# An attention and DFT kernel: eleven spectral blocks beside attention instead of ten, a thinner output projection, and more tiles for loads

## The chip, the cores and the metric

The kernel runs on one core of a Trainium2 chip. The metric is the device time of one launch in microseconds. The engines are TensorE (PE, with PEld for its weight loads), VectorE (DVE), ScalarE (ACT), GpSimd (POOL) and SyncE (SP), which here issues nearly all DMAs. Each engine runs its own instructions in the order in which the kernel emits them; a DMA that has to wait for a buffer holds up whatever stands behind it in its issuer's queue.

## The reference

Two mixers see the same `x` (2048 rows of 512), and a gate adds them:

```python
qkv = x @ wqkv                                  # 32 heads of 16
p = softmax(q @ k.T * 16 ** -0.5)               # 2048 x 2048 per head
a = (p @ v).reshape(2048, 512) @ wo
b = dft_seq_re @ (x @ dft_hid_re.T) - dft_seq_im @ (x @ dft_hid_im.T)
g = sigmoid((x * gate_w).sum(-1))
out = g * a + (1 - g) * b
```

All of it is float32. The weights of the attention are large, so the softmax needs a row maximum that is right before the exponentials are taken, and products are made from a high and a low part of each operand (three matmuls for one product).

## The kernel before

**Two parts.** The *front* makes the projections (q, k, v), the two hidden DFTs and most of the DFT along the sequence ("spectral" blocks), and beside them part of the *scans*: matmuls of q and k whose only result is the row maximum. The second part is *attention*, 512 steps (16 pairs of heads, two halves of the queries, 16 blocks of keys). Each step makes scores (`qk`, L214), exponentials on ACT (L238 for the first half of the columns, L246 twice for the second) and the products with the values (`pv`, L758).

**What fills the steps of attention.** A step has room for other work on PE. Step 2 to step `MIX - 1` hold one scan each (`next_scan`). From `MIX` on, `next(fill)` runs the generator `outputs()`: first `LATER` spectral blocks of the second DFT half, 16 steps each with three pairs of matmuls a step (`spectral`); then the output projection `mix_heads` for 16 row blocks t, each in two steps (4 and 5 pairs) or, for even t below `2 * SLOW`, in four (2, 2, 2, 3 pairs); then twelve steps of `mix_some`. There are 1024 scans in all; `FRONT` of them are made in the front, so `MIX = TOTAL - FRONT + 1`. Step numbers below are these steps; a step's place in its pair of heads is called i, as in the code (0 to 31).

**Slots.** Every product in the front is a pair of matmuls on the two halves of the PE rows (`halves_of`, L189), and after each the kernel calls `beside()`. One such call is a *slot*. Twelve slots make one projection, or a quarter u of a spectral block. The front before has 80 projections and 88 quarters (`coef`: 64 of the first DFT half, 24 of the second), 2016 slots. `beside` adds `1 / pace` per slot and emits a scan whenever the sum reaches one: `PACE`, `SUMS` in the projections, `BESIDE` once folding has begun, `PART` in the spectral part, `SWAP` at its start and where the DFT half changes. `after(n, f)` emits work n slots later, which is how the casts, the stores and the loads are spread.

**Scans in the front.** From scan 64 on they are folded (`scan_folded`, L158): for one half of the keys ACT takes `Relu` of the difference of two key blocks (L162), for the other DVE adds it and takes the maximum (L164). Each uses one of four PSUM banks, so a late ACT or DVE stops PE at the next scan with that bank. The order of pairs is `SEQ`: the ten pairs of `EARLY`, then the first `FRONT % 64` scans of `PART_PAIR` (11), then pair 10. The rows of a pair (q and k, two tiles of the pool `stk`, which has six buffers) are loaded by eight DMAs, seven slots apart, when the scan listed in `ROWS` is reached.

**The swap of operands.** The spectral products read operands `ah[s]`, `al[s]`, s = 0 to 15. During t = 15 of the first half (four quarters of `coef`, slots 1656 to 1680 and 1704 to 1728) each is replaced by the second half's: `renew(s)` casts the raw operand on ACT (L701), then a subtraction on DVE or POOL follows, and for s >= 8 the next raw operand is ordered (`load_operand`, L342, tag `raw`). The raw operands 0 to 7 come in two `stk` tiles named `early`, ordered from slot 1584 on. The coefficients of quarter n are loaded by `fetch` (L361, tag `craw`) and split on POOL by `prepare` three quarters ahead (L368, L369).

**Near the end of the front**, eight quarters before its last, the rows of `PART_PAIR` are loaded once more for the scans of attention, and those of pair 0 for `qk` (`load_use`). In attention `load_use(p + 1)` comes at i = 18 and `load_scan` ten scans before a pair's last. `output_rows(c)` loads the heads' results for four row blocks of the output projection, `load_y(c)` the rows of the spectral sum that they are added to.

Of the kernel before, what the change touches and what calls it, by code (L numbers as in the profile page):

```python
# [10 lines left out]
F32 = mybir.dt.float32  # L11
# [7 lines left out]
P = 128  # L19
S = 2048  # L20
D = 512
# [3 lines left out]
NB = S // P  # L25
# [4 lines left out]
CS = 4  # L30
NU = NB // CS
PERIODS = 2 * NB
SCANS = 64
TOTAL = SCANS * NP
LATER = 10
FRONT = 564 + 16 * LATER
FOLDED = range(SCANS, FRONT)
PACE, SUMS, BESIDE, PART, SWAP = 3.9, 5.2, 2.72, 2.07, 2.97
PART_PAIR = FRONT // SCANS
EARLY = [0, 4, 5, 6, 7, 1, 2, 3, 8, 9]  # L40
SEQ = [(p, i) for p in EARLY for i in range(SCANS)]
SEQ += [(PART_PAIR, i) for i in range(FRONT % SCANS)] + [(p, i) for p in range(len(EARLY), PART_PAIR) for i in range(SCANS)]
SEQ += [(n // SCANS, n % SCANS) for n in range(FRONT, TOTAL)]
ROWS = {SCANS * n + (20 if n else 40): p for n, p in enumerate(EARLY[1:])}
ROWS.update({SCANS * len(EARLY) - 60: PART_PAIR, SCANS * len(EARLY) - 34: len(EARLY)})
NWARM = 20
MIX = TOTAL - FRONT + 1
OUT = MIX + NB * LATER
SLOW = 3
SCANS_IN = 0  # L50
AHEAD = (30, 31, 37, 44)


def build(tc, xT, wqkv, wo, wrT, wiT, cr, ci, gate, out):
    nc = tc.nc
    with ExitStack() as ctx:
# [176 lines left out]
        def qk_both(p, h, kb):  # L233

            ps = wide(1 - SCANS_IN, "s3")
            qk(p, h, kb, 0, [ps[:, j, :] for j in range(2)])
# [18 lines left out]
        with ExitStack() as pf:  # L255
# [36 lines left out]
            def beside():  # L292
# [5 lines left out]
                pace[1] += 1.0 / pace[0]  # L298
                while seen[0] < FRONT and pace[1] >= 1.0:
                    pace[1] -= 1.0  # L300
# [37 lines left out]
                engine.tensor_sub(lo, raw, hi.bitcast(F32))  # L338

            def load_operand(ph, s, pool):  # L340
                raw = pool.tile([P, D], F32, tag="raw", name="abr", bufs=3)
                nc.sync.dma_start(raw, ab_d[ph][s])  # L342
                return raw

# [6 lines left out]
            for ph, plain, pair in ((0, range(NB - 2), (NB - 2, NB - 1)), (1, range(2, NB), (0, 1))):  # L351
                split_up = [(ph, t, u) for half in range(2) for t in pair for u in (2 * half, 2 * half + 1)]
                whole = [(ph, t, u) for t in plain for u in range(NU)]
                coef += split_up + whole if ph else whole + split_up
            coef = coef[:len(coef) - NU * LATER]
            craw, ready = {}, {}

            def load_coef(n, raw):
                ph, t, u = coef[n]
                craw[n] = raw  # L360
                nc.sync.dma_start(raw, (cr, ci)[ph][t, :, u * CS:(u + 1) * CS, :])  # L361
# [273 lines left out]
            with ExitStack() as py:  # L635
                cp = py.enter_context(tc.tile_pool(name="cp", bufs=2, reuse_waits="tile"))
                def fetch(n):
                    if n < len(coef):
                        load_coef(n, cp.tile([P, CS, P], F32, tag="craw", name="craw", bufs=5))

                for n in range(4, 8):
                    fetch(n)
                for d in range(4):
                    after(4 + 6 * d, split_operand, NB - 4 + d, tail[:, d, :], nc.gpsimd)
                scan_at(SWAP)
                after(24, scan_at, PART)
                pss, yre, early = {}, {}, {}

                def go_ahead(k):

                    if k == 0:
                        assert seen[0] == FRONT, (seen, pace)
                        scanned.update(unfolded)
                        sums.append(narrow("k1", "pvb"))
                        nc.vector.memset(sums[0], 0.0)
                    if k == 1:
                        e = next_eb()
                        ahead.append(qk_single(0, 0, 0, [e[:, j, :] for j in range(2)]))
                    elif k == 2:
                        scan(seen[0], wide(1 - SCANS_IN, "s1"))  # L660
                        seen[0] += 1
                    else:
                        ahead.append(qk_both(0, 0, k // 3))

                def mixed(ph, t, yre, tx, ty):
                    y = cp.tile([P, D], F32, tag="y", name="y")
                    nc.gpsimd.tensor_add(y, tx, ty)
                    if ph:
                        nc.gpsimd.tensor_add(y, y, yre)
                    after(14, nc.sync.dma_start, y_d[t // 4][:, t % 4, :], y)  # L670

                for n, (ph, t, u) in enumerate(coef):
                    prepare(n + 3)
                    fetch(n + 8)
                    if u == 0 and (ph, t) == (0, NB - 1):
                        scan_at(SWAP)
                    if u == 2 and (ph, t) == (1, 0):
                        scan_at(PART)
                    if n == len(coef) - 2 * NU:
                        unfolded[PART_PAIR], loads = row_loads(PART_PAIR, nc.sync)  # L680
                        for load in loads:
                            load()
                        load_use(0)
                    hi, lo = ready.pop(n)
                    if u == 0:
                        pss[t] = xy()
                        if ph:
                            yre[t] = cp.tile([P, D], F32, tag="yre", name="yre")
                            nc.sync.dma_start(yre[t], y_d[t // 4][:, t % 4, :])
                    if (ph, t, u) == (0, NB - 3, 0):  # L690
                        for i in range(2):
                            raw = stk.tile([P, 4, D], F32, tag="stk", name="early")
                            for d in range(4):
                                early[4 * i + d] = raw[:, d, :]
                                after(24 * i + 6 * d, nc.sync.dma_start, raw[:, d, :], ab_d[1][4 * i + d])
                    swap = (ph, t) == (0, NB - 1)

                    def renew(s):
                        raw = early.pop(s)
                        ah[s], al[s] = block(2 * s), block(2 * s + 1)  # L700
                        nc.scalar.copy(ah[s], raw)  # L701
                        after(4, (nc.gpsimd if s % 4 == 3 else nc.vector).tensor_sub, al[s], raw, ah[s].bitcast(F32))
                        if s >= 8 and s + 3 < NB:
                            early[s + 3] = load_operand(1, s + 3, cp)

                    for w in range(CS):
                        s = u * CS + w
                        for i, (c_, a_) in enumerate(((hi, ah[s]), (hi, al[s]), (lo, ah[s]))):
                            halves_of(pss[t], c_[:, w, :], a_, s == 0 and i == 0, s == NB - 1 and i == 2)
                            beside()  # L710
                            if n >= len(coef) - NU and 3 * s + i in AHEAD:
                                go_ahead(AHEAD.index(3 * s + i))
                        if swap:
                            if s == 7:
                                for i in range(8, 11):
                                    early[i] = load_operand(1, i, cp)
                            after(1 + 5 * (s % 8), renew, s)
                    if u == NU - 1:
                        tx = cp.tile([P, D], F32, tag="tx", name="tx")
                        last = n == len(coef) - 1  # L720
                        ty = cp.tile([P, D], F32, tag="raw" if last else "ty", name="ty", bufs=3 if last else 2)
                        if last:
                            for v, ps in zip((tx, ty), pss[t]):
                                nc.vector.tensor_scalar_mul(v, ps, gm[:, t:t + 1])
                        else:
                            nc.scalar.mul(tx, pss[t][0], gm[:, t:t + 1])
                            after(5, nc.scalar.mul, ty, pss[t][1], gm[:, t:t + 1])
                        after(10, mixed, ph, t, yre.get(t), tx, ty)
                run_due((True, True))

        assert seen[0] == FRONT + 1 and turns[0] % 2 == SCANS_IN, (seen, turns)

        with ExitStack() as pa:
# [12 lines left out]
            def pair_banks():  # L746
                return wide(SCANS_IN, "s1")

# [109 lines left out]

            raws, units = [], [(t, u) for t in range(NB - LATER, NB) for u in range(NU)]
            parts = []  # L860
# [84 lines left out]
            def outputs():  # L945

                for t in range(NB - LATER, NB):
                    yield from spectral(t)
                for c in range(NC):
                    for t in range(4 * c, 4 * c + 4):  # L950
                        yield from mix_heads(t, (2, 2, 2, 3) if t < 2 * SLOW and t % 2 == 0 else (4, 5))
                    if c < 2:
# [41 lines left out]
            for step in range(NP * PERIODS):  # L994
                p, i = step // PERIODS, step % PERIODS
# [120 lines left out]
```

## Time and profile before

| | us |
|---|---|
| median of 3 runs | 1736.33 |
| lowest, highest | 1735.86, 1737.74 |
| the profiled execution | 1736.52 |
| its span in the profile | 1734.7 |

In the profile the front ends at about 670 us, the scans in attention at about 1245 us, the spectral blocks beside attention at about 1597 us. Rows of stretches give, after the stretch and its length, each engine's busy time with its number of instructions, then the clock of TensorE, the share of the DMA engines and GB/s. In rows of waits stand the total, the count and the longest wait; in rows of the chain the start, the length, and the engine with its line; in rows of the timeline the start, the length, and in brackets the idle time before with what ended it.

### The profile page before, as it was taken

The numbers are of one execution on the slowest core, as the hardware profiler recorded it, in microseconds if no ns is written. First come the engines' busy times: TensorE is split into PE (matmuls) and PEld (weight loads), VectorE is DVE, ScalarE is ACT, GpSimd is POOL, SyncE is SP. The second block draws the span as 40 slices with busy tenths as digits, with TensorE's granted clock in tenths as the row PEclk, the third lists the DMA queues.
The fourth block names the chain that finished last, engine by engine and source line by source line (L and its number), as shares of the span: only waits on it lengthen the run. The fifth ranks groups of instructions, "written<-read, shape, count | busy, mean of one in ns | idle before, by whom it ended". The sixth has DMA issues, their size and how long they took to land.

```text
span 1734.7 us, 36067 instructions
## 1 busy us (share of the span) xinstructions
PE 1718.8 (99%) x13676; PEld 1045.2 (60%) x13676; DVE 1094.3 (63%) x2065; ACT 1507.4 (87%) x2487; POOL 648.9 (37%) x770
## 2 busy tenths in 40 slices
PE   9999999999999999999999999999999999999998
PEld 7978888889888786433333333333455555555554
DVE  6898888899999897666666666666512222122333
ACT  5447888888888788999999999999988888888885
POOL 3673335755555662223323232332322322223221
PEclk9999999999999999999999999999999999999999
DMA  7783457433336746043333332351333244254712
GB/s 255 243 279 75 147 159 214 141 108 115 105 114 192 160 117 114 21 84 62 61 61 64 59 75 51 56 100 43 60 86 92 68 115 89 67 149 138 177 36 99
DMA packets 123710, 193.03 MB, mean 111 GB/s; under 512 B 54112, under 2 KB 56656, under 8 KB 116624
## 3 DMA queue, kind: packets, MB, share of 16 engines
q1 hardware_dynamic: 84464, 170.20, 37.3%
q0 software_dynamic: 38496, 19.47, 5.5%
q8 instruction: 107, 1.75, 0.5%
q10 hardware_dynamic: 576, 1.05, 0.2%
q14 instruction: 67, 0.55, 0.1%
HBM read 129.63 MB, written 61.61 MB: 110 GB/s over the span
## 4 chain that ended last, share of the span: by engine, by line
PE 94%; POOL 1%; DMA 1%; issue 1%; ACT 1%; DVE 1%; SPq 0%; DVEq 0%; POOLq 0%; ACTq 0%
PE pvb L758 28%; PE xy L189 23%; PE s L214 19%; PE s L189 10%; PE s L158 9%; PE s L139 5%; POOL s L282 1%; DMA abr<-ab_d 0%; POOL el L282 0%; ACT fold L162 0%; DMA raws<-wqkv 0%; DVE fold L164 0%; DVE y L856 0%; PE s L556 0%; ACT eh L282 0%
## 5 line engine op out<-in xcount | busy, mean ns | idle before, releaser
L238 ACT ACTIVATE eb<-s 128x1024 f32<-128x1024 f32 x512 | 575.6, 1124 | 65.7 <-PE s L214 65.4
L246 ACT ACTIVATE e<-s 128x512 f32<-128x512 f32 x1022 | 605.6, 702 | 0.4 <-PE s L214 0.4
L141 DVE TENSOR_REDUCE mx<-s 128x2 f32<-128x1024 f32 x364 | 442.5, 1225 | 188.9 <-PE s L139 188.7
L758 PE MATMUL pvb<-eb,va 128*17 128x512 f32 x2052 | 513.0, 597 | 0.0
L758 PE MATMUL pvb<-e,va 128*17 128x512 f32 x2044 | 512.1, 597 | 0.0
L164 DVE CUSTOM_DVE_ANT_0 fold<-s,fold 128x512 f32<-128x512 f32 x660 | 442.6, 690 | 57.4 <-PE s L158 20.3
L162 ACT ACTIVATE fold<-s 128x512 f32<-128x512 f32 x660 | 387.4, 603 | 74.7 <-PE s L158 52.0
L214 PEld LDWEIGHTS s<-qs,ks 50*128 50x128 f32 x2048 | 211.9, 184 | 355.6 <-ACT eb L238 255.1
L214 PE MATMUL s<-qs,ks 50*128 50x512 f32 x2048 | 420.0, 434 | 0.0
L189 PE MATMUL xy<-b,c 64*128 64x512 f32 x2448 | 400.6, 393 | 1.0 <-ACT s L478 0.7
L158 PE MATMUL s<-ks,qs 48*128 48x512 f32 x1320 | 323.3, 406 | 4.3 <-ACT fold L162 3.1
L189 PEld LDWEIGHTS xy<-b,c 64*128 64x128 f32 x2448 | 288.2, 187 | 17.1 <-ACT s L478 2.8
L158 PEld LDWEIGHTS s<-ks,qs 48*128 48x128 f32 x1320 | 178.2, 184 | 52.4 <-ACT fold L162 13.9
L777 POOL DMA_DIRECT2D r_d<-lc x31 | 18.1, 583 | 456.5 <-DVE lc L776 456.5
L758 PEld LDWEIGHTS pvb<-eb,va 128*17 128x17 f32 x2052 | 70.5, 96 | 192.3 <-issue 185.1
L139 PE MATMUL s<-ks,qs 48*128 48x512 f32 x728 | 151.2, 395 | 0.7 <-DVE mx L141 0.7
L770 POOL DMA_DIRECT2D lc<-ob x124 | 62.9, 514 | 154.9 <-DVE ob L767 154.5
L189 PE MATMUL xy<-w,b 64*128 64x512 f32 x768 | 116.9, 393 | 0.2 <-ACT s L478 0.2
L369 POOL TENSOR_TENSOR c<-craw,c 128x512 fp32r<-128x512 f32 x84 | 110.6, 1317 | 6.7
L189 PE MATMUL s<-b,chi 64*128 64x512 f32 x670 | 105.9, 392 | 0.3 <-ACT chi L1071 0.3
L368 POOL CAST c<-craw 128x512 fp32r<-128x512 f32 x84 | 51.9, 618 | 126.6 <-PE xy L189 121.6
L189 PEld LDWEIGHTS xy<-w,b 64*128 64x128 f32 x768 | 83.9, 186 | 11.0 <-ACT s L478 1.1
(138 smaller groups left out, 1478.8 us busy)
## 6 DMA issues: line engine op xcount, KB each, us to landing
qs<-q_d SPq DMA_DIRECT2D x66, 256.0 KB
craw<-ci SPq DMA_DIRECT2D x64, 256.0 KB
craw<-cr SPq DMA_DIRECT2D x60, 256.0 KB
ks<-k_d SPq DMA_DIRECT2D x44, 256.0 KB
qs<-q_d SPq DMA_DIRECT2D x66, 128.0 KB
ab_d<-ab SPq DMA_DIRECT2D x32, 256.0 KB
y_d<-y SPq DMA_DIRECT2D x32, 256.0 KB
o_d<-oh POOLq DMA_DIRECT2D x28, 256.0 KB, 13.6
```

The lines of the kernel that those rows point to most:

```text
L139: nc.tensor.matmul(ps[:, j, :], qs[b:b + 48, qb * P:(qb + 1) * P], ks[b:b + 48, c * 512:(c + 1) * 512], start=True, stop=True)
L141: nc.vector.tensor_reduce(mx[p][:, :, qb, c], ps, axis=AX.X, op=ALU.max)
L158: nc.tensor.matmul(ps, qs[b:b + 48, qb * P:(qb + 1) * P], ks[b:b + 48, c * 512:(c + 1) * 512], start=True, stop=True)
L162: nc.scalar.activation(fold[j], ps, AF.Relu)
L164: nc.vector.tensor_tensor_reduce(out=fold[j], in0=ps, in1=fold[j], scale=1.0, scalar=-3.0e38, op0=ALU.add, op1=ALU.max, accum_out=mx[p][:, ...
L189: nc.tensor.matmul(ps[j], lhs[r], rhs[r], start=first, stop=last)
L214: nc.tensor.matmul(pss[j], ks[b:b + 50, kb * P:(kb + 1) * P], qs[b:b + 50, q0:q0 + 512], start=True, stop=True)
L238: nc.scalar.activation(e, ps, AF.Exp, scale=SCALE)
L246: nc.scalar.activation(e[j], pss[j], AF.Exp, scale=SCALE)
L369: sub(lo, raw, hi.bitcast(F32))
L758: nc.tensor.matmul(pvb[r:r + VC, :], va[:, kb, 2 * p + j, :], es[c][j], start=kb == 0, stop=kb == NB - 1, tile_position=(0, r))
L770: nc.gpsimd.dma_start(lc[32 * n:32 * n + 32, :], ob[r + DH:r + VC, :].rearrange("p (s e) -> p s e", e=16))
```

## The change

`LATER` goes from 10 to 11: block t = 5 of the second DFT half is made in attention. `SLOW` goes from 3 to 6: the row blocks t = 6, 8 and 10 of `mix_heads` take four steps. `FRONT` becomes 558 + 176 + 12 = 746 (before: 724), so 22 more scans are made in the front and `MIX` is 279 instead of 301; the output projection starts at step 455 instead of 461. The front has 84 quarters instead of 88, 1968 slots. `BESIDE`, `PART` and `SWAP` are smaller. The rows of pair 10 are asked for 18 scans before the end of `EARLY`'s scans instead of 34, which with the new paces is slot 1664 instead of 1728; those of pair 11 (scan 580 in both) come at slot 1580 instead of 1653. `SCANS_IN` swaps the two wide PSUM tiles, because the front now uses the two in turn once less. Raw operands of the second half get five tiles instead of three and are ordered five ahead, five of them from s = 3 to 7 of the swap; coefficients get seven tiles instead of five and are fetched ten quarters ahead instead of eight.

```diff
-LATER = 10
-FRONT = 564 + 16 * LATER
+LATER = 11
+SLOW = 6
+FRONT = 558 + 16 * LATER + 2 * SLOW
 FOLDED = range(SCANS, FRONT)
-PACE, SUMS, BESIDE, PART, SWAP = 3.9, 5.2, 2.72, 2.07, 2.97
+PACE, SUMS, BESIDE, PART, SWAP = 3.9, 5.2, 2.5, 1.945, 2.9
...
-ROWS.update({SCANS * len(EARLY) - 60: PART_PAIR, SCANS * len(EARLY) - 34: len(EARLY)})
+ROWS.update({SCANS * len(EARLY) - 60: PART_PAIR, SCANS * len(EARLY) - 18: len(EARLY)})
...
-SLOW = 3
-SCANS_IN = 0
+SCANS_IN = 1
...
-                raw = pool.tile([P, D], F32, tag="raw", name="abr", bufs=3)
+                raw = pool.tile([P, D], F32, tag="raw", name="abr", bufs=3 if ph == 0 else 5)
...
-                        load_coef(n, cp.tile([P, CS, P], F32, tag="craw", name="craw", bufs=5))
+                        load_coef(n, cp.tile([P, CS, P], F32, tag="craw", name="craw", bufs=7))
 
-                for n in range(4, 8):
+                for n in range(4, 10):
                     fetch(n)
...
-                    fetch(n + 8)
+                    fetch(n + 10)
...
-                        if s >= 8 and s + 3 < NB:
-                            early[s + 3] = load_operand(1, s + 3, cp)
+                        if s >= 8 and s + 5 < NB:
+                            early[s + 5] = load_operand(1, s + 5, cp)
...
-                            if s == 7:
-                                for i in range(8, 11):
-                                    early[i] = load_operand(1, i, cp)
+                            if 3 <= s < 8:
+                                early[s + 5] = load_operand(1, s + 5, cp)
...
-                        ty = cp.tile([P, D], F32, tag="raw" if last else "ty", name="ty", bufs=3 if last else 2)
+                        ty = cp.tile([P, D], F32, tag="raw" if last else "ty", name="ty", bufs=5 if last else 2)
```

## The prediction

> **What bounds the kernel now.** First the page's busy line, then a table of stretches, then single groups in those stretches, because the page's 99% for PE hides that the stages have different limits.
>
> ```profile
> span 1734.7 us, 36067 instructions
> PE 1718.8 (99%) x13676; PEld 1045.2 (60%) x13676; DVE 1094.3 (63%) x2065; ACT 1507.4 (87%) x2487; POOL 648.9 (37%) x770
> ```
>
> The stretches are: projections without scans, the first DFT half with folded scans, the swap of operands, the rest of the front, attention beside scans, attention beside spectral blocks, attention beside the output projection.
>
> ```profile
> core 0: us, PE busy (x) PEld busy (x) DVE busy (x) ACT busy (x) POOL busy (x), PEclk, DMA share, GB/s
> 40.00:80.00 40.00, 40.00 (x350) 36.08 (x348) 30.31 (x30) 19.15 (x36) 23.23 (x18) 1.00 0.70 229
> 344.00:540.00 196.00, 196.00 (x1642) 173.56 (x1640) 180.36 (x543) 167.16 (x294) 103.03 (x107) 1.00 0.42 122
> 560.00:600.00 40.00, 37.04 (x301) 29.81 (x299) 33.69 (x90) 31.13 (x56) 26.43 (x24) 1.00 0.83 181
> 600.00:660.00 60.00, 59.98 (x502) 51.30 (x500) 55.77 (x167) 51.31 (x92) 37.08 (x37) 1.00 0.52 117
> 720.00:1220.00 500.00, 500.00 (x3696) 188.62 (x3688) 338.52 (x313) 500.00 (x793) 155.98 (x233) 1.00 0.34 64
> 1260.00:1580.00 320.00, 320.00 (x2636) 169.04 (x2632) 63.51 (x108) 285.20 (x440) 84.45 (x126) 1.00 0.39 100
> ```
>
> In the front every matmul comes as a pair of row halves. 350 matmuls in 40 us are 0.2286 us per pair without scans; 1642 in 196 us are 0.2387 us per pair with them. So PE bounds the front, one pair after another. In the swap 301 matmuls take 40 us where 150.5 pairs at 0.2387 need 35.9: about 4.1 us are lost there, the one real stall of the front. Beside scans in attention ACT is busy for all of its 500 us, and an attention step holds 14 matmuls against 18 beside a spectral block, though PE reads 100% in both. The groups of scans (L158), folds (L164) and first exponentials (L238, one per step) give the prices:
>
> ```profile
> 344.00:540.00 196.00, 128.94 (x536) 72.34 (x534) 1.00 0.42 122
> 344.00:540.00 196.00, 179.35 (x535) 1.00 0.42 122
> 720.00:1220.00 500.00, 313.78 (x265) 1.00 0.34 64
> 1260.00:1580.00 320.00, 151.01 (x146) 1.00 0.39 100
> ```
>
> 268 scans of two matmuls lie among the 821 pairs of 344 to 540 us: with the other 553 at 0.2286, a scan costs (196 - 126.4)/268 = 0.26 us. A scan step of attention takes 500/264 = 1.894 us (265 less the cut ends), a spectral step 320/146 = 2.19 us.
>
> The output projection, by the chain of work (one row for two steps):
>
> ```profile
> 1607.10 1.84 PE pvb L758 x16
> 1611.47 1.84 PE pvb L758 x16
> 1615.86 1.84 PE pvb L758 x16
> 1620.86 1.84 PE pvb L758 x16
> ...
> 1644.82 1.84 PE pvb L758 x16
> 1649.89 1.84 PE pvb L758 x16
> ```
>
> A block spread over four steps (2, 2, 2, 3 pairs) takes two intervals of 4.37 and 4.39 us, 8.76 us together; a block in two steps (4, 5) takes one interval of 5.00 to 5.07 us. With 4 or 5 pairs the interval is as long as with a spectral block's 6, so thinning the work below that buys nothing.
>
> **The change, part by part.**
>
> *The front loses block t=5 of the second half.* 16 x 3 = 48 pairs: 48 x 0.2286 = -10.97 us. It gains 22 scans: 22 x 0.26 = +5.72 us. Sum -5.3; with all 26 pairs of difference at the mixed 0.2387 it is -6.2. I take -5.7, since the removed pairs stood among scans. With the block go its preparation on POOL, its evacuation on ACT and four coefficient loads on SP, all of them beside PE.
>
> *Attention.* 22 scan steps go (-22 x 1.894 = -41.7), 16 spectral steps come (+16 x 2.19 = +35.0), and t = 6, 8, 10 of the output projection take four steps for two (+3 x (8.76 - 5.07) = +11.1). Sum +4.4. The six longer steps alone nearly cancel with six scan steps (11.1 against 11.4); the block is what costs. The spectral block's own splits and sums lie on DVE, which is busy for 63.5 of 320 us there, its four coefficient loads on SP at a DMA share of 0.39: nothing, with that cover.
>
> *Denser scans in the front.* BESIDE 2.72 to 2.5, PART 2.07 to 1.945, SWAP 2.97 to 2.9. At PART a scan comes every 2.945 pairs, 0.703 us. DVE's folds are busy 179.35/268 = 0.67 us per scan, 95% of that against 91% before. But the profile's busy time holds a fixed tail:
>
> ```profile
> 582.52 0.68 DVE L164 CUSTOM_DVE_ANT_0 fold<-s,fold 128x512 f32<-128x512 f32 x1
> 583.13 0.08 DVE L164 DVE_READ_ACCUMULATOR2_ANT mx<- 128x1 f32 x1
> 583.13 0.68 DVE L164 CUSTOM_DVE_ANT_0 fold<-s,fold 128x512 f32<-128x512 f32 x1
> ```
>
> Back to back a fold starts every 0.61 us, so 0.09 us per scan are still free. Between nothing and 3 us (a fold's 0.61 us late five times) I take +0.3.
>
> *The swap: more operand tiles, other row loads.* Here the stall of now is seen, in the chain of work, the DMA issues with their sizes, ACT's timeline and SP's waits.
>
> ```profile
> 567.14 2.25 DMA craw<-ci
> ...
> 580.84 7.90 DMA abr<-ab_d
> ```
>
> ```profile
> craw<-ci SPq DMA_DIRECT2D x64, 256.0 KB
> ...
> qs<-q_d SPq DMA_DIRECT2D x66, 128.0 KB
> ```
>
> ```profile
> 582.91 0.60 ACT L162 ACTIVATE fold<-s 128x512 f32<-128x512 f32 x1 [1.04 <-PE s L158]
> 585.14 0.62 ACT L701 CAST b<-abr 128x512 fp32r<-128x512 f32 x1 [1.64 <-DMA abr<-ab_d]
> 585.67 1.08 ACT L162 ACTIVATE fold<-s 128x512 f32<-128x512 f32 x2
> 588.77 0.62 ACT L701 CAST b<-abr 128x512 fp32r<-128x512 f32 x1 [2.02 <-DMA abr<-ab_d]
> ```
>
> ```profile
> SPq L342 <- DVE b L282: 8.2, 4, 3.3
> ```
>
> With three tiles an operand is fetched only when the one three before it has been split: SP waits 8.2 us for that, the load then takes 7.90 us, and ACT's cast stands in front of the folds that free PE's banks (waits of 1.64 and 2.02 us). Five tiles order operand s five ahead, two renewals earlier: this stall's cause goes. Seven coefficient tiles do the same for coefficients, but each fetch still takes the tile that was just prepared, so SP waits on POOL as often.
>
> What is late next: the rows of pair 10. Counting slots, they are asked for at slot 1664 (scan 622) instead of 1728 (scan 606). At 1664 all six `stk` buffers are held: pair 9's rows until scan 639 (slots 1714 to 1717), pair 11's rows, and the two `early` tiles until the last renewal of s<8 (slot 1720); at 1728 the `early` tiles were free. So the first load waits on SP until the first `early` tile is read (about slot 1690), the second until about slot 1717. Behind it stand the loads of operands 9 to 12, wanted by ACT from slot 1716 on, and the coefficient fetches. Then 14 transfers of 256 or 128 KB go at once, 3200 KB up to operand 13; at the 181 GB/s of the swap's row above this is 18.1 us, where operand 13 is due after 32 slots (32 x 0.2286 + 11 scans x 0.26 = 10.2 us). From below, all 4.1 us of stall go. From above, 2.25 us for operand 9 (a lone load's time, the first row above) and 7.9 us for operand 13 take their place: +6.1. Pair 11's rows have left the swap for an earlier place, which speaks for the lower part of that: I take -1.0.
>
> *Late in attention.* The rows of `y` for the last eight blocks:
>
> ```profile
> 1637.25 0.83 SPq L851 DMA_DIRECT2D y<-y_d  x2
> 1642.77 3.75 SPq L838 DMA_DIRECT2D b<-o_d  x6
> ```
>
> Now `y` goes first and the six loads of `output_rows(3)` follow at step 483. With the longer blocks `output_rows(3)` is issued at step 479, ahead of `y` at 480: 3.75 us of issue more, and 1.5 MB ahead in the queue, while the sum of t = 8 is due after one block of 8.76 us. Bounds 0 and 2 us; I take +0.2. The row loads of attention meet a buffer shortage too (scans now change pairs at i = 23, after `load_use` at i = 18), but nine steps of 1.894 us are left for them: 0.
>
> *Sum.* -5.7 + 4.4 + 0.3 - 1.0 + 0.2 = -1.8 us. The profiled execution took 1736.52 us, 1.82 over its span, and lies 0.19 over the median of 1736.33: about 1734.5 us.
>
> **The rivals.**
>
> *Faster: the swap runs without a stall.* For it: five tiles and rows of pair 11 out of the way. Against it: six held `stk` buffers. Then -5.7 + 4.4 + 0.3 - 4.1 = -5.1, with -6.2 for the front -5.6: about 1731 us.
>
> *Slower: the held row load starves ACT.* SP waits in front of operands 9 to 15, ACT's cast waits for them, folds wait behind it, PE's banks fill. It makes the kernel slower by over 3.5 us once the swap stalls 4.3 us longer than now, 8.4 us in all; at the upper bound the sum is -5.7 + 4.4 + 0.5 + 6.1 = +5.3, 1741.6 us. For it: 7.90 us for one operand load already now. Against it: fewer row loads fall into the swap.
> [...]
>
> *No change: PE is the bound everywhere.* PE is busy 500.00 of 500.00 us beside scans, so a matmul might cost there what it costs in the front; moving 26 pairs would then be even: -5.7 + 26 x 0.2387 = +0.5, without stalls moved 1737 us. Against it: 14 matmuls a step beside scans, 18 in a spectral one at only 1.16 times the time.
> [...]
>
> **How the numbers follow.** A difference under 0.2%, 3.5 us, is what a measurement of this kernel can hardly tell from none. My forecast holds 0.39, the even exchange 0.05, the faster rival 0.35, the slower one 0.16, and 0.05 go to a delay that no term holds. The forecast and the exchange lie within 0.2% (0.42 of their 0.44); most of the faster rival lies beyond it. That gives faster 0.37, same 0.42, slower 0.21. The range reaches from 1729.0, the faster rival's 1730.7 less 1.7 (should the deeper prefetch take most of that lone coefficient load's 2.25 us off the chain too), to the slower one's 1741.6; the likeliest case alone spans 1733 to 1738.
>
> **What would show it.** Front: the last folded scan about 5 us earlier less the swap's change. Attention: still near 1.89 and 2.19 us per step, eight-plus-microsecond pairs of intervals for six blocks. Swap: fewer matmuls missing than now if the stall went; if SP's row loads (L104) wait some 15 us there, and ACT's casts (L701) again wait for `abr`, the held buffers did it. DVE's wait at t = 8 (L856) for `y` would show the late load. I am wrong if folds make PE wait throughout the front, or if a step's price beside scans changes.

## The result, and the profile after

The changed kernel is slower, and outside the predicted range.

| us | before | after |
|---|---|---|
| median (6 runs each) | 1736.28 | 1747.73 |
| lowest, highest | 1735.60, 1737.74 | 1746.92, 1751.12 |
| span of the profiled execution | 1734.7 | 1745.3 |
| first exponential of attention (L238), from the trace | 670.8 | 678.1 |
| from there to the end | 1063.9 | 1067.2 |

The ratio is 1.0067, interval 1.0056 to 1.0077. Attention is 3.3 us longer where 4.4 were forecast. The front, forecast 6.4 us shorter, is 7.3 us longer. The front alone is 13.7 us off, and that is the miss.

Four of the stretches of the prediction, of the kernel after (stretch, its length, each engine's busy time with its number of instructions, TensorE clock, DMA share, GB/s):

```profile
344.00:540.00 196.00, 196.00 (x1614) 169.83 (x1612) 182.99 (x559) 170.71 (x300) 99.20 (x104) 1.00 0.38 108
560.00:600.00 40.00, 36.67 (x286) 30.18 (x285) 33.83 (x91) 30.65 (x57) 23.58 (x23) 0.96 0.55 143
720.00:1220.00 500.00, 499.91 (x3698) 192.81 (x3700) 334.78 (x318) 499.03 (x790) 152.31 (x229) 1.00 0.34 66
1260.00:1580.00 320.00, 320.00 (x2636) 169.16 (x2637) 63.14 (x112) 285.19 (x440) 87.21 (x126) 1.00 0.43 101
```

The two attention rows have the counts of before (3698 against 3696 matmuls, 2636 against 2636). The front has not: 1614 matmuls against 1642 in 344 to 540 us although PE reads 196.00 in both, 286 against 301 in the swap, and the clock column of that row is 0.96 where it was 1.00. As in the prediction, the count shows what PE's busy time does not.

To place the loss I count by slots, not by time, because the same slot lies at other times in the two kernels. The start of the first matmul of slots 457, 960, 984, 1656 and 1776 is read from the trace; from each stretch 0.2286 us per slot and 0.253 us per scan are taken off. The second is an estimate of a scan that waits for nothing: in the spectral part of before half of the scans cost at most 0.248 us, and with that in its place no difference below would move by more than about 0.1 us. What is left is waiting:

| waiting, us | slots | before | after | more |
|---|---|---|---|---|
| projections with folded scans | 457-960 | 3.7 | 8.5 | 4.8 |
| spectral part | 984-1656 | 2.5 | 6.4 | 3.9 |
| swap | 1656-1776 | 5.9 | 8.7 | 2.8 |

With the pairs and scans themselves (-48 x 0.2286 + 22 x 0.253 = -5.4) that is +6.1 of the front's +7.3; the other 1.2 us are waits elsewhere in it, 0.8 of them behind the swap.

**Where PE waits.** The waits of PE's weight loads, first the projections (before: 137 to 302 us, after: 137 to 311 us; line, what it waited for, total us, times, longest). Before:

```profile
PEld s L158 <- ACT fold L162: 3.8, 10, 0.8
PEld s L158 <- DVE mx L164: 3.3, 14, 0.4
```

After:

```profile
PEld s L158 <- ACT fold L162: 7.0, 15, 0.5
PEld s L158 <- DVE mx L164: 6.0, 26, 0.5
```

Then the spectral part, before (310 to 548 us):

```profile
PEld s L158 <- DVE mx L164: 3.6, 18, 0.3
```

and after (320 to 568 us):

```profile
PEld s L158 <- DVE mx L164: 7.3, 28, 0.4
```

All of these are scans that wait for the bank of an earlier scan, none longer than 0.8 us. DVE's maxima are waited for 54 times in the two parts where it was 32 times. ACT's folds cost more waiting in the projections alone; in the spectral part their waits do not grow (3.5 us before, 3.0 after). In the spectral part the place can be seen. `PART` = 1.945 puts most scans two slots apart, but 19 of the 346 only one slot apart, which before never happens there. One such place in PE's and PEld's timelines of after (start, length, engine, line, idle before it with its cause):

```profile
351.47 0.47 PE L158 MATMUL s<-ks,qs 48*128 48x512 f32 x2
351.71 0.47 PE L189 MATMUL xy<-b,c 64*128 64x512 f32 x2
352.06 0.50 PE L158 MATMUL s<-ks,qs 48*128 48x512 f32 x2
```

```profile
352.06 0.19 PEld L158 LDWEIGHTS s<-ks,qs 48*128 48x128 f32 x2 [0.32 <-DVE mx L164]
```

One pair (x2) stands between the scans at 351.47 and 352.06 where otherwise two or more stand, and the second scan waits 0.32 us for DVE. A slot with its scan takes 0.648 us in these places and 0.483 where scans are two slots apart: 19 x 0.165 = 3.1 us.

**The swap.** SP's queue in 550 to 610 us of after, by waits and then by its issues of row loads (L104) and operand loads (L342); L282 is the line that runs what `after` put off, here the subtractions:

```profile
SPq L104 <- PE s L158: 7.1, 1, 7.1
SPq L104 <- DVE b L282: 6.8, 1, 6.8
SPq L104 <- POOL b L282: 2.4, 1, 2.4
```

```profile
578.83 0.55 SPq L104 DMA_DIRECT2D ks<-kf_d  x1
...
587.63 0.33 SPq L104 DMA_DIRECT2D qs<-q_d  x1
588.00 1.37 SPq L342 DMA_DIRECT2D abr<-ab_d  x3
```

These waits of L104 add up to 16.3 us; the prediction's last part named some 15 as the sign of this case. The first row load is held until the `early` tile is split (DVE, POOL: L282), the second until scan 639 has read pair 9's rows; three operand loads issued behind it only at 588.00 are what ACT needs next. ACT's casts after:

```profile
591.35 0.62 ACT L701 CAST b<-abr 128x512 fp32r<-128x512 f32 x1 [3.35 <-DMA abr<-ab_d]
...
604.67 0.62 ACT L701 CAST b<-abr 128x512 fp32r<-128x512 f32 x1 [1.90 <-DMA abr<-ab_d]
```

and PE's timeline, where the first stop is DVE's and the second follows from the cast above:

```profile
587.40 0.86 PE L189 MATMUL xy<-b,c 64*128 64x512 f32 x6
589.64 0.68 PE L158 MATMUL s<-ks,qs 48*128 48x512 f32 x2 [1.38 <-DVE mx L164]
589.98 0.81 PE L189 MATMUL xy<-b,c 64*128 64x512 f32 x4
592.51 0.56 PE L158 MATMUL s<-ks,qs 48*128 48x512 f32 x2 [1.72 <-ACT fold L162]
```

Then something that neither the prediction nor a rival has. Stretches of 4 us of after:

```profile
588.00:592.00 4.00, 1.41 (x10) 0.71 (x6) 2.29 (x7) 0.66 (x3) 3.92 (x4) 1.00 0.85 256
592.00:596.00 4.00, 3.49 (x18) 2.77 (x20) 3.24 (x10) 2.65 (x5) 0.03 (x1) 0.60 1.07 253
596.00:600.00 4.00, 4.00 (x36) 3.08 (x34) 2.58 (x8) 3.54 (x7) 3.21 (x4) 0.97 1.04 233
```

After the two stops the clock granted to TensorE is 0.60 and 0.97. As one stretch at half speed that is (0.40 x 4 + 0.03 x 4) / 0.5 = 3.4 us, and the trace's own record of the clock has it so: 0.50 from 592.81 us on, for 3.41 us. With PE busy for 3.49 of the 4 us from 592 and for all of the next 4, half of that, about 1.7 us, is my estimate of what it costs.

### The profile page after: what moved, and what is told of

It reads as the page before. It is cut to its first block, busy times and chain, and to the rows that moved or that the text cites. A ratio compares the mean times of both kernels' runs of the same rounds, so it can differ in the third digit from the quotient of the medians.

```text
span 1745.3 us, 36160 instructions
## 1 busy us (share of the span) xinstructions
PE 1727.6 (99%) x13676; PEld 1033.6 (59%) x13676; DVE 1084.7 (62%) x2097; ACT 1518.3 (87%) x2507; POOL 641.4 (37%) x760
## 4 chain that ended last, share of the span: by engine, by line
PE 92%; issue 2%; POOL 2%; DMA 2%; ACT 1%; DVE 1%; SPq 0%; DVEq 0%; POOLq 0%; ACTq 0%
PE pvb L757 28%; PE xy L189 21%; PE s L214 18%; PE s L158 10%; PE s L189 10%; PE s L139 4%; POOL s L282 1%; ACT fold L162 1%; POOL el L282 0%; DVE fold L164 0%; DMA q_d<-eh 0%; DMA raws<-xT 0%; DMA raws<-wqkv 0%; ACT ty L506 0%; DVE y L855 0%
## 5 line engine op out<-in xcount | busy, mean ns | idle before, releaser
L238 ACT ACTIVATE eb<-s 128x1024 f32<-128x1024 f32 x512 | 574.6, 1122 | 67.8 <-PE s L214 67.8
L141 DVE TENSOR_REDUCE mx<-s 128x2 f32<-128x1024 f32 x342 | 415.5, 1224 | 175.3 <-PE s L139 175.1
L757 PE MATMUL pvb<-eb,va 128*17 128x512 f32 x2052 | 511.0, 597 | 0.0
L757 PE MATMUL pvb<-e,va 128*17 128x512 f32 x2044 | 510.1, 597 | 0.0
L164 DVE CUSTOM_DVE_ANT_0 fold<-s,fold 128x512 f32<-128x512 f32 x682 | 454.7, 690 | 51.4 <-ACT fold L162 17.9
L162 ACT ACTIVATE fold<-s 128x512 f32<-128x512 f32 x682 | 398.5, 603 | 70.9 <-PE s L158 45.9
L189 PE MATMUL xy<-b,c 64*128 64x512 f32 x2352 | 395.6, 394 | 0.9 <-ACT s L478 0.7
L158 PE MATMUL s<-ks,qs 48*128 48x512 f32 x1364 | 343.1, 412 | 6.2 <-DVE mx L164 2.9
L189 PEld LDWEIGHTS xy<-b,c 64*128 64x128 f32 x2352 | 273.8, 187 | 19.7 <-ACT s L478 2.8
L158 PEld LDWEIGHTS s<-ks,qs 48*128 48x128 f32 x1364 | 186.1, 184 | 67.3 <-DVE mx L164 20.6
L757 PEld LDWEIGHTS pvb<-eb,va 128*17 128x17 f32 x2052 | 71.5, 96 | 192.7 <-issue 183.4
L139 PE MATMUL s<-ks,qs 48*128 48x512 f32 x684 | 137.7, 394 | 0.1
L189 PE MATMUL s<-b,chi 64*128 64x512 f32 x734 | 115.6, 391 | 0.3 <-ACT chi L1070 0.3
L873 DVE CAST chi<-craw 128x512 fp32r<-128x512 f32 x44 | 18.9, 430 | 147.2 <-PE s L189 147.2
L369 POOL TENSOR_TENSOR c<-craw,c 128x512 fp32r<-128x512 f32 x80 | 104.5, 1307 | 6.4
```

The lines of the kernel that those rows point to most:

```text
L139: nc.tensor.matmul(ps[:, j, :], qs[b:b + 48, qb * P:(qb + 1) * P], ks[b:b + 48, c * 512:(c + 1) * 512], start=True, stop=True)
L141: nc.vector.tensor_reduce(mx[p][:, :, qb, c], ps, axis=AX.X, op=ALU.max)
L158: nc.tensor.matmul(ps, qs[b:b + 48, qb * P:(qb + 1) * P], ks[b:b + 48, c * 512:(c + 1) * 512], start=True, stop=True)
L162: nc.scalar.activation(fold[j], ps, AF.Relu)
L164: nc.vector.tensor_tensor_reduce(out=fold[j], in0=ps, in1=fold[j], scale=1.0, scalar=-3.0e38, op0=ALU.add, op1=ALU.max, accum_out=mx[p][:, ...
L189: nc.tensor.matmul(ps[j], lhs[r], rhs[r], start=first, stop=last)
```

## The experiments

Each kernel changes either the kernel before or the kernel after, as its diff says. Ratios are against the kernel before, timed on the same chip. Waiting by slots, as above, of the profiled execution of each:

| us of waiting | projections | spectral | swap | first exponential at |
|---|---|---|---|---|
| before | 3.7 | 2.5 | 5.9 | 670.8 |
| after | 8.5 | 6.4 | 8.7 | 678.1 |
| e1 rows late | 8.6 | 6.4 | 4.5 | 674.6 |
| e2 buffers | 3.9 | 2.4 | 2.8 | 667.3 |
| e3 `BESIDE` 2.5 | 8.6 | 2.3 | 4.3 | 674.3 |
| e4 `PART` 1.945 | 3.9 | 7.4 | 10.5 | 684.2 |
| e5 `PART` 2.0 | 3.8 | 3.7 | 3.5 | 670.4 |
| e9 `BESIDE` 2.6 | 6.8 | 1.6 | 7.3 | 674.8 |
| e10 ten blocks, even | 1.3 | 1.7 | 4.4 | 668.0 |
| e12 eleven blocks, even | 8.5 | 4.0 | 4.6 | 671.6 |

**The swap: rows later, and buffers alone.** The kernel after, with the rows of pair 10 ordered at scan 644, when the `early` tiles and pair 9's rows are free:

```diff
-ROWS.update({..., SCANS * len(EARLY) - 18: len(EARLY)})
+ROWS.update({..., SCANS * len(EARLY) + 4: len(EARLY)})
```

> The changed kernel, with the rows of pair 10 asked for at scan 644 (slot 1726, when the early tiles are free) instead of scan 622 (slot 1664). Theory of the held row load: SP no longer waits for a buffer in the swap, operands 9 to 15 come in time, TensorE's clock does not fall after a long stop; the swap loses 1 to 3 us instead of 8.4, so the time is 5 to 7 us under the changed kernel's 1747.7, about 1742. Rival, too many bytes for the DMA engines in the swap: the row loads now fall on operands 13 to 15, the loss only moves, 1746 to 1750.

Measured: 1743.34, ratio 1.0045 (1.0032 to 1.0057), 4.4 us under the changed kernel's median, in other runs. The swap's waiting falls from 8.7 to 4.5, more than the 1 to 3 expected to be left, and the stretch of 560 to 600 us reads

```profile
560.00:600.00 40.00, 37.95 (x311) 31.42 (x309) 36.45 (x99) 33.10 (x63) 27.23 (x25) 1.00 0.57 158
```

311 matmuls against 286, clock 1.00. Some 4 us of the loss therefore come from the place of one pair's row loads, the slower clock behind the stop included.

The kernel before, with only the tiles and earlier loads:

```diff
-                raw = pool.tile([P, D], F32, tag="raw", name="abr", bufs=3)
+                raw = pool.tile([P, D], F32, tag="raw", name="abr", bufs=3 if ph == 0 else 5)
...
-                        load_coef(n, cp.tile([P, CS, P], F32, tag="craw", name="craw", bufs=5))
+                        load_coef(n, cp.tile([P, CS, P], F32, tag="craw", name="craw", bufs=7))
-                for n in range(4, 8):
+                for n in range(4, 10):
...
-                    fetch(n + 8)
+                    fetch(n + 10)
...
-                        if s >= 8 and s + 3 < NB:
-                            early[s + 3] = load_operand(1, s + 3, cp)
+                        if s >= 8 and s + 5 < NB:
+                            early[s + 5] = load_operand(1, s + 5, cp)
...
-                            if s == 7:
-                                for i in range(8, 11):
-                                    early[i] = load_operand(1, i, cp)
+                            if 3 <= s < 8:
+                                early[s + 5] = load_operand(1, s + 5, cp)
...
-                        ty = cp.tile([P, D], F32, tag="raw" if last else "ty", name="ty", bufs=3 if last else 2)
+                        ty = cp.tile([P, D], F32, tag="raw" if last else "ty", name="ty", bufs=5 if last else 2)
```

> The kernel before, with nothing but the larger tile counts: five raw operands, seven coefficients, and their earlier loads. Rows of pair 10 stay at slot 1728, where buffers are free. Theory: ACT no longer waits for operands 14 and 15, the 4.1 us of stall between 560 and 600 us shrink to 1 or less, 1732 to 1733. Rival, the DMA engines' rate is what makes the operands late: all requests come earlier but land as late, 1735 to 1737.

Measured: 1733.32, ratio 0.9984 (0.9975 to 0.9993), the best kernel of this study, ahead of both given ones, and just above the 1732 to 1733 expected. Its swap:

```profile
560.00:600.00 40.00, 39.30 (x323) 31.76 (x319) 35.81 (x97) 33.96 (x63) 27.96 (x26) 1.00 0.80 183
```

323 matmuls against 301 before. So this part of the change does what it says, and is worth some 3 us (5.9 to 2.8); in the changed kernel the early row loads more than take it back.

**The scans: one pace at a time.** The kernel before, with `BESIDE` alone (the rows of pair 10 moved to stay at their slot):

```diff
-PACE, SUMS, BESIDE, PART, SWAP = 3.9, 5.2, 2.72, 2.07, 2.97
+PACE, SUMS, BESIDE, PART, SWAP = 3.9, 5.2, 2.5, 2.07, 2.97
-ROWS.update({..., SCANS * len(EARLY) - 34: len(EARLY)})
+ROWS.update({..., SCANS * len(EARLY) - 18: len(EARLY)})
```

> The kernel before, with BESIDE 2.5 instead of 2.72 alone (the rows of pair 10 asked for at scan 622, which is slot 1728 as before). The same scans, earlier. Theory of density: in the projections (slots 457 to 960) PE waits more for ACT and DVE, as in the changed kernel, where the stretch costs 4.7 us over the price of its pairs; 3 to 5 us slower, 1740. Rival, by the prediction's small term, a busy DVE with slack: within 1 us of before.

Measured: 1738.26, ratio 1.0017 (1.0008 to 1.0026). The projections wait 8.6 us, as in the changed kernel; the swap, whose scans lie elsewhere now, gives 1.6 us back, so the total moves less than expected. What DVE and ACT do in the projections beside folds shows why 0.7 us per scan is too little there, by their groups in 137 to 311 us of the kernel after (busy us and mean ns after the first bar, idle before them after the second):

```profile
L164 DVE CUSTOM_DVE_ANT_0 fold<-s,fold 128x512 f32<-128x512 f32 x200 | 135.4, 689 | 22.0 <-ACT fold L162 8.8 <-PE s L158 8.6
L609 DVE TENSOR_TENSOR ab<-tx,xy 128x512 f32<-128x512 f32 x20 | 13.7, 683 | 0.2
```

```profile
L501 ACT ACTIVATE tx<-xy 128x512 f32<-128x512 f32 x42 | 25.0, 596 | 2.3 <-PE xy L189 2.3
L506 ACT ACTIVATE ty<-xy 128x512 f32<-128x512 f32 x16 | 9.7, 604 | 0.0
```

Beside 200 folds DVE does these 20 sums of 0.68 us, each as long as a fold (and six more at L587), and ACT evacuates the banks of the products (L501, and L506 behind it where POOL makes the sum). A scan two slots after the last one leaves 2 x 0.2286 + 0.253 = 0.71 us, some 0.1 more than a fold takes on DVE, so there is no room for such an operation. The waits listed above can be followed to them in the trace. Each of the 15 waits for ACT ended with a fold that stood directly behind an evacuation (12 times L506, twice L501) or, once, a cast, as only 51 of ACT's 201 folds do. Each of the 26 waits for DVE ended with a fold in an unbroken run of DVE's work with such a sum (24 times) or a reduction of maxima (L179, twice) close before it, as only 57 of its 200 folds do. In the spectral part 27 of DVE's 28 waits have nothing but folds before them.

With 2.6, a value between (the rival was a beat of the pace with the slots that 2.5 alone would have):

```diff
-PACE, SUMS, BESIDE, PART, SWAP = 3.9, 5.2, 2.72, 2.07, 2.97
+PACE, SUMS, BESIDE, PART, SWAP = 3.9, 5.2, 2.6, 2.07, 2.97
-ROWS.update({..., SCANS * len(EARLY) - 34: len(EARLY)})
+ROWS.update({..., SCANS * len(EARLY) - 25: len(EARLY)})
```

> The kernel before, with BESIDE 2.6 instead of 2.72 (rows of pair 10 at scan 615). 2.5 cost 4.8 us of waits in the projections (slots 457 to 960). Theory of density: 2.6 costs about half of that, 2 to 2.5 us. Rival, the beat of 2.5, where scans come two and three slots apart in turn so that all even scans (ACT's) follow after two and all odd ones (DVE's) after three: 2.6 breaks the turn, under 1 us.

Measured: 1738.99, ratio 1.0019 (1.0010 to 1.0027), with 3.1 us more waiting in the projections (2 to 2.5 were expected): between 0 at 2.72 and 4.8 at 2.5, so the cost grows with the number of scans two slots apart (51 at 2.72, 100 at 2.5) and is no beat. The swap waits 1.4 us more here than in the kernel before and 1.6 less in e3; it answers to where its scans fall, which I did not separate.

`PART` alone at 1.945, in the kernel before:

```diff
-PACE, SUMS, BESIDE, PART, SWAP = 3.9, 5.2, 2.72, 2.07, 2.97
+PACE, SUMS, BESIDE, PART, SWAP = 3.9, 5.2, 2.72, 1.945, 2.97
-ROWS.update({..., SCANS * len(EARLY) - 34: len(EARLY)})
+ROWS.update({..., SCANS * len(EARLY) - 13: len(EARLY)})
```

> The kernel before, with PART 1.945 instead of 2.07 alone (the rows of pair 10 asked for at scan 627, slot 1726). Theory of scans one slot apart: a pace under 2 sets a scan directly behind the scan of the slot before about every 18th time, and such a one takes 0.65 us in the changed kernel's trace where the others take 0.48; with some 22 of them 3 to 4 us slower, 1740. Rival, DVE's slack of 0.09 us per scan is enough: within 1 us of before.

Measured: 1746.47, ratio 1.0067 (1.0055 to 1.0080): right in direction, some 6 us too small. The spectral part waits 4.9 us more, with 19 scans one slot apart again; the swap, which here has three operand tiles, 4.6 us more. In the profiled execution, 3.9 us above the kernel's median, the clock falls too:

```profile
600.00:604.00 4.00, 3.31 (x18) 1.90 (x20) 2.21 (x7) 1.87 (x4) 0.76 (x2) 0.69 0.99 210
604.00:608.00 4.00, 4.00 (x20) 3.11 (x22) 2.37 (x9) 1.39 (x4) 0.96 (x2) 0.50 1.06 178
608.00:612.00 4.00, 4.00 (x35) 3.28 (x35) 3.18 (x11) 3.24 (x6) 1.49 (x2) 0.96 0.78 159
```

(0.31 + 0.50 + 0.04) x 4 / 0.5 = 6.8 us at half speed, after an idle of PE of 1.78 us at a scan and with another of 0.65 in it. Three of its five executions have a mean clock of 0.999 against 0.997 here, so it does not happen each time.

`PART` at 2.0, where no two scans are one slot apart:

```diff
-PACE, SUMS, BESIDE, PART, SWAP = 3.9, 5.2, 2.72, 2.07, 2.97
+PACE, SUMS, BESIDE, PART, SWAP = 3.9, 5.2, 2.72, 2.0, 2.97
-ROWS.update({..., SCANS * len(EARLY) - 34: len(EARLY)})
+ROWS.update({..., SCANS * len(EARLY) - 23: len(EARLY)})
```

> The kernel before, with PART 2.0 instead of 2.07 (rows of pair 10 at scan 617, about slot 1726). Every scan of the spectral part is then exactly two slots behind the last, never one. Theory of scans one slot apart: between slots 984 and 1584 the loss stays near the 2.0 us of before (6.5 with 1.945), no long stop in the swap, TensorE's clock stays at 1; time within 1.5 us of before. Rival, density: 2.0 is more than halfway from 2.07 to 1.945, so about 5 to 6 us slower.

Measured: 1736.79, ratio 1.0007 (0.9999 to 1.0016); the spectral part waits 3.7 us with 336 scans against 7.4 with 345 at 1.945. Nine scans fewer, half the waiting: in the spectral part it is the scans one slot apart, not the mean pace.

**Fewer thin blocks.** The kernel after with `SLOW` at 3, and so six scans fewer in the front and six steps fewer in the output projection, to measure that trade by itself:

```diff
-SLOW = 6
+SLOW = 3
```

> The changed kernel, with SLOW 3 as before (FRONT 740). By the prediction's prices three row blocks fall from 8.76 to 5.07 us (-11.1), six scan steps of 1.894 us come back (+11.4) and six scans leave the front (-1.5): 1 to 1.5 us under the changed kernel, 1746 to 1747. Rival, the longer blocks relieve the end of attention by more than these prices say: slower than the changed kernel.

Measured: 1800.49, ratio 1.0375 (1.0361 to 1.0388). The expectation missed by over 50 us; the rival had the direction, but not this reason. The loss is in attention, in four steps with i = 29 (steps 29, 93, 157 and 221), which take 14.5 to 14.9 us each in place of 1.9. The chain of waits at the first of them, step 29 (start, length, what):

```profile
731.94 0.27 PE s L214 x2
732.22 0.32 SPq L104
...
735.82 8.37 DMA qs<-q_d
...
744.32 0.76 PE s L139
```

and the clock around it:

```profile
734.00:738.00 4.00, 0.00 (x0) 0.00 (x0) 0.00 (x0) 0.89 (x1) 0.03 (x1) 0.91 1.13 203
738.00:742.00 4.00, 0.76 (x1) 0.29 (x1) 0.00 (x0) 0.00 (x0) 2.23 (x3) 0.50 1.04 178
742.00:746.00 4.00, 1.68 (x7) 0.65 (x11) 0.88 (x1) 0.45 (x1) 2.53 (x3) 0.50 0.15 18
746.00:750.00 4.00, 4.00 (x22) 0.98 (x14) 1.77 (x4) 2.52 (x5) 0.00 (x0) 0.50 0.27 61
750.00:754.00 4.00, 4.00 (x28) 1.38 (x28) 1.87 (x3) 2.79 (x5) 0.00 (x0) 0.89 0.19 59
```

`FRONT` mod 64 sets at which i the scans of attention change their pair: i = 13 before (724), 23 after (746), 29 here (740). At 29 the next pair's rows are ordered at i = 19, just behind `load_use` at i = 18, with the pool's six buffers taken; SP issues them only when the last scan of the old pair is done, and the next scan waits, by the chain, for seven issues of 0.32 to 0.58 us and then 8.37 us of transfer. `SLOW` is thus no independent number: it moves `FRONT` by two each. The prediction's "nine steps are left" was true for 746 and says nothing of its neighbours.

`SLOW` at 5 keeps the order of the two loads (change of pair at i = 25):

```diff
-SLOW = 6
+SLOW = 5
```

> The changed kernel with SLOW 5: FRONT 744, so the scans of attention change pairs at i = 25 and their rows are asked for at i = 15, ahead of load_use at i = 18 (with SLOW 3 it was i = 29 and i = 19, behind it, and every second pair of heads stopped for 14.5 us at i = 29). Theory of the order of the two loads: no such stop, 1746 to 1749, within 2 us of the changed kernel. Rival, fewer thin row blocks as such cost time: between the changed kernel and SLOW 3's 1800, 1760 or more.

Measured: 1755.92, ratio 1.0113 (1.0098 to 1.0129), between the 1746 to 1749 expected and the rival's 1760. No step of 14.5 us is left, which agrees with that cause, but two other places are slow now: steps of 5.65 and 3.22, and of 5.51 and 3.12 us, at i = 12 and the step behind it. DVE's timeline at the first:

```profile
765.30 0.25 DVE L775 RECIPROCAL lc<-lc 128x16 f32<-128x16 f32 x1 [2.76 <-DMA lc<-ob]
765.47 1.16 DVE L141 TENSOR_REDUCE mx<-s 128x2 f32<-128x1024 f32 x1
```

The reciprocal of the softmax sums waits 2.76 us for a small DMA, and the reduction of a scan waits behind it. Ten blocks with the buffers of e2 and `SLOW` at 0 show the same at i = 28:

```diff
-FRONT = 564 + 16 * LATER
+FRONT = 558 + 16 * LATER
-SLOW = 3
+SLOW = 0
```

> The kernel before with the larger tile counts (as e2_buffers) and with SLOW 0: FRONT 718, all sixteen row blocks in two steps, the output projection from step 467. By the same prices: three blocks -11.1, six scan steps +11.4, six scans fewer in the front -1.5, on e2_buffers' 1733.3: about 1732. Rival: no difference from e2_buffers.

Measured: 1739.74 (1732.72 to 1744.19), ratio 1.0022 (1.0009 to 1.0034), against about 1732 expected and 1733.32 with `SLOW` at 3, in other runs. DVE's timeline:

```profile
905.88 0.25 DVE L775 RECIPROCAL lc<-lc 128x16 f32<-128x16 f32 x1 [3.31 <-DMA lc<-ob]
```

That the large row loads in flight delay that small DMA fits the places in both kernels, but no run took the row loads away alone, so it is argued and not shown. The fewer thin blocks of e8 gain nothing that could be seen beside this.

**Can either be made better?** Ten blocks with e2's buffers, scans moved from the projections to the spectral part:

```diff
-PACE, SUMS, BESIDE, PART, SWAP = 3.9, 5.2, 2.72, 2.07, 2.97
+PACE, SUMS, BESIDE, PART, SWAP = 3.9, 5.2, 2.95, 2.0, 2.97
-ROWS.update({..., SCANS * len(EARLY) - 34: len(EARLY)})
+ROWS.update({..., SCANS * len(EARLY) - 36: len(EARLY)})
```

> The kernel before with the larger tile counts (e2_buffers), BESIDE 2.95 and PART 2.0, rows of pair 10 at scan 604 (slot 1728): fewer scans in the projections, where they made PE wait, more in the spectral part, where two slots apart cost hardly more than 2.07. Theory: the projections lose 1.5 us or so less than the 3.7 of before, the rest stays as in e2_buffers: 1731 to 1733. Rival, a loss in the projections that does not hang on the scans' density: as e2_buffers, 1733 to 1734, or worse by the 0.8 us that PART 2.0 showed.

Measured: 1734.89, ratio 0.9997 (0.9988 to 1.0006), 2 us above what was expected. The projections wait 1.3 us in place of 3.9, somewhat better than expected, but slots 960 to 984 wait 2.4 in place of 0.6, and the swap 4.4 in place of 2.8: given back.

Eleven blocks, with rows late, no scans one slot apart, and the scans that are left over in the swap:

```diff
-PACE, SUMS, BESIDE, PART, SWAP = 3.9, 5.2, 2.5, 1.945, 2.9
+PACE, SUMS, BESIDE, PART, SWAP = 3.9, 5.2, 2.5, 2.0, 2.5
-ROWS.update({..., SCANS * len(EARLY) - 18: len(EARLY)})
+ROWS.update({..., SCANS * len(EARLY) + 1: len(EARLY)})
```

> The changed kernel with the rows of pair 10 at scan 641 (slot 1729), PART 2.0 and SWAP 2.5, so that all 746 scans still fit and none is one slot behind another. Theory: against e1_rows_late (1743.3) the 4 us that the spectral part lost to such scans go, the denser swap gives 0 to 2 back: 1739 to 1741, still 3 to 5 us over before, because the projections keep their 4.8 us. Rival, what the changed kernel loses there is DVE's load and not the spacing: 1742 to 1744.

Measured: 1740.66, ratio 1.0030 (1.0018 to 1.0041), as expected and 7.1 us under the changed kernel's median, in other runs. The swap falls to 4.6, the spectral part to 4.0; the projections keep their 8.5. What stays above the kernel before is about their 4.8.

## Why the prediction was wrong

*Attention, +4.4: right.* Measured +3.3. By the starts of L238 a step beside scans takes 1.898 us (forecast 1.894), one beside a spectral block 2.188 (2.19). The blocks in four steps, by the chain of waits of after:

```profile
1606.67 1.84 PE pvb L757 x16
1611.05 1.84 PE pvb L757 x16
1615.42 1.84 PE pvb L757 x16
1620.49 1.84 PE pvb L757 x16
```

4.38, 4.37 and 5.07 us per two steps, as priced.

*Late `y`, +0.2, and attention's row loads, 0: right.* At the steps of t = 8 the starts are 4.37, 4.37 and 5.01 us apart, so nothing waits. The row loads cost nothing at 746; e6 shows how near that is to steps of 14.5 us.

*Front pairs, -5.7: right.* By pairs and scans without waits it is -5.4; the waits come on top.

*"Between nothing and 3 us (a fold's 0.61 us late five times) I take +0.3": wrong, and the largest part of the miss.* The runs show +4.8 in the projections (e3 alone has it) and +3.9 in the spectral part (e4 has +4.9, e5 with `PART` 2.0 has +1.2). Two errors lie in that step. It took the mean spacing, 0.703 us at `PART`, and set it against a fold's 0.61 us; but a scan falls on whole slots, and at 1.945 one in 18 comes after 0.2286 + 0.253 = 0.48 us, shorter than a fold, and waits (0.648 us a slot against 0.483). And it priced `PART` only, where DVE does little beside folds; in the projections DVE's sums and ACT's evacuations lie between the folds, and every wait there leads back to such an operation.

*The swap, -1.0: wrong; the slower rival's mechanism happened.* SP waited in front of operands at L104, ACT's cast waited 3.35 and 1.90 us for `abr`, PE stopped. The term measured +2.8, inside its bounds (-4.1 to +6.1); about 1.7 of it, by the estimate above, is the clock, which was in no bound. The buffers alone give about -3 (e2), the row loads at their place take that and more (8.7 against 4.5 in e1), so "fewer row loads fall into the swap" was no help where some of them were held. The rival's own time, 1741.6, needed that stall alone at its upper bound; the kernel went past it with a smaller one and the folds' waits together.

*The faster rival* needed a swap without stall; e2 still has 2.8 us. *The even exchange* is refuted by attention's step prices, 1.898 and 2.188 us. *"I am wrong if folds make PE wait throughout the front"* is what came.

Without the waits the exchange itself would be -5.4 + 3.3 = -2.1 us. What it takes is 22 more scans in 48 fewer slots, and the waits for folds that this brings, 4.8 + 3.9 = 8.7 us, are four times as much.

## What to carry to other kernels

A consumer that keeps up on average does not keep up with work that is placed on whole slots: compare its time with the shortest spacing that the pace makes, count how often that comes, and do so in every stage with that stage's other work on the consumer. Before ordering a load earlier, find out which buffers are free at that place: in the changed kernel's swap a row load that waited on SP's queue kept the three operand loads behind it until 588.00 us. And where one number sets the total of a periodic sequence, write down what else it moves, as here the place where pairs change.

## What the runs showed of the hardware

**Half clock after stops.** TensorE's granted clock fell to 0.50 after stops and stayed there for 3.4 us (after), 6.8 us (e4), and (0.09 + 0.50 + 0.50 + 0.50 + 0.11) x 4 / 0.5 = 13.6 us (e6, from within a stop of two idles, 6.47 and 3.48 us, on). In e8 and e11 the matmuls behind the longer stops in attention ran slower as well: rows of L757 that take 0.61 us ahead of the stop take up to 1.07 us behind an idle of 2.44 (e8) and 1.06 us behind one of 1.86 (e11), and the mean clock of the profiled execution is 0.997 and 0.994. In the kernel before and in e1, e2 the clock stayed at 1.00 through the swap. So in these runs a stall had a second price that came after it, about 1.7 us for the shortest by the estimate above. It is not the length of a stop alone: after fell with idles of 1.38 and 1.72 us that ended 2.9 us apart, e9 kept the full clock through one nearly twice as long. PE's timeline of e9 and its stretches there:

```profile
592.01 0.50 PE L158 MATMUL s<-ks,qs 48*128 48x512 f32 x2 [3.12 <-ACT fold L162]
596.80 0.50 PE L158 MATMUL s<-ks,qs 48*128 48x512 f32 x1 [1.48 <-ACT fold L162]
```

```profile
588.00:592.00 4.00, 0.89 (x8) 0.40 (x4) 0.25 (x3) 1.16 (x3) 0.17 (x1) 1.00 1.07 201
592.00:596.00 4.00, 3.31 (x25) 2.54 (x25) 2.51 (x7) 1.41 (x3) 2.01 (x2) 1.00 1.01 168
596.00:600.00 4.00, 3.20 (x28) 2.69 (x30) 2.71 (x8) 3.22 (x7) 2.42 (x3) 1.00 1.08 197
```

Nor does PE's busy time in these stretches tell them apart: PE was busy for 0.89 of the 4 us from 588 to 592 in e9, which stayed at 1.00, and for 1.41 of the 4 us from 588 to 592 in after, ahead of the fall. What sets a stop that loses the clock apart from one that keeps it is not shown.

**A long subtraction on DVE beside a long sum on POOL.** Ahead of the first of the two stops in after (and of one of 1.38 us that is left in e1, where the longest such subtraction takes 1.80) stands a DVE subtraction of 1.78 us; the row before it has the same work in 0.69:

```profile
586.59 0.69 DVE L282 TENSOR_TENSOR b<-early,b 128x512 fp32r<-128x512 f32 x1
587.20 1.78 DVE L282 TENSOR_TENSOR b<-abr,b 128x512 fp32r<-128x512 f32 x1
```

POOL's timeline in the same place:

```profile
586.60 1.83 POOL L667 TENSOR_TENSOR y<-tx,ty 128x512 f32<-128x512 f32 x1 [1.06 <-ACT ty L282]
```

POOL's sum of two tiles, whose median is 1.30 us, begins with DVE's first subtraction and takes 0.53 longer; DVE's second subtraction ends 0.55 us after POOL's sum. No run moved the one away from the other, so why both took longer is not shown. In the swap of before such subtractions took up to 1.60 us, so it is not new with the change; what it costs in either kernel is not shown.
